# Second mixture of a fused attention and mixture kernel: the sixteen tiles of the seven-product form, in groups of four, four and eight in place of eight and eight

## The chip, the core and the metric

One core of one Trainium2 chip runs the whole program in one launch. The metric is the device time in microseconds (us) of that launch, from the first instruction to the last. TensorE is written PE (its weight loads PEld), VectorE DVE, ScalarE ACT, GpSimd POOL, and the queue of the sync engine SP.

## What is computed

Three stages follow each other: an attention with a feature map, a mixture in which each token goes to one of eight experts, and a second mixture in which every token goes through all four experts. The change touches the last one, which is this:

```python
def _moe2_ref(x, domain_probs, w1, w2) -> np.ndarray:
    N, D = x.shape                       # 2304, 512
    E = w1.shape[0]                      # 4; w1 is (4, 512, 1024), w2 is (4, 1024, 512)
    p = domain_probs / (domain_probs.sum(-1, keepdims=True) + 1e-09)
    out = np.zeros((N, D), dtype=np.float32)
    for e in range(E):
        h = np.maximum(x @ w1[e], 0.0)
        out += p[:, e:e + 1] * (h @ w2[e])
    return out.astype(np.float32)
```

## The kernel before

Tokens stand in 18 tiles of 128 rows. Every float32 operand is split into two float16 parts, hi and lo, and a product of two operands is three matmuls (hi·hi, hi·lo, lo·hi). The first layer of an expert can be done in two forms. Tiles 0 and 1 ("few") take the plain form, `few_l1` (matmuls at L1578, 256 columns). The other sixteen take a form with seven products of half-sized blocks in place of eight: tiles are paired, one from the first half of a group and one from the second, and from each pair seven block operands are made (`x2_two`), split in hi and lo, and turned by DMA transposes into `xq` (L1527). A group is a list of first tiles and a list of second tiles; before, there are two groups, tiles 2 to 9 and tiles 10 to 17, four tile pairs each (`GT = 4`), so a matmul of the form (L1595) has 512 columns.

An expert e runs as a list of units: the few unit, then one unit per group (`run_few`, `run_pair`). In a group's unit four steps j = 0 to 3 each issue the seven products of `pair_l1` (seven times six matmuls), and behind step j stands the second layer of step j - 1 for the group's first tiles (`l2_a`, L1638 with `ha`); the second tiles follow at the end (`l2_all`, L1638 with `hb`, 24 matmuls a tile), and each finished tile goes through `out_tile` (L1628 for expert 0, L1630 after). ACT copies the first product out of PSUM (L1601); DVE adds the others (L1603 to L1620); the hidden layer is rectified on ACT (L1567) and its low part made on DVE (L1568). Products rotate through four PSUM buffers (`psf`), so PE can stand four products ahead of the engines that empty them.

The order of the instructions on each engine is that of the code, and every engine takes its own in that order. Three things are interleaved with the units by counting: `x2.step(n)` advances the making of the next group's operands by n steps, `conv2.step(n)` advances the splitting of the expert's weights, and `x2.drain()` at the start of a unit puts all steps that are left there at once. Steps of `x2_pair` are taken in the few unit by the list `pace`, and in the first group's unit of expert 0 at each yield of `l2_a` (one or two steps in turn, one yield a tile and step j) and of `l2_all` (two steps, one yield a tile, behind the tile's `out_tile`). One tile pair takes six steps: norms on ACT (L160), scale factors on DVE (L166 to L170), scaling and the first split (L153, L1540 on ACT; L156, L1543, L1545, L1546 on DVE; a transpose of the operands A), the sums (L1549, L1550), and the second split (L1548, L1552 on ACT; L1553, L1555 on DVE; a transpose of the operands S). The first two tile pairs of the first group have norms and scales done earlier (`x2_norms`, `EARLY = 2`). The products of a step take operands in the order A11, A12, S2, S1, S3, S4, A22. A tile pair's operands need two `raw` buffers of six; weights wait in the same buffers.

## Time and profile before

| | us |
|---|---|
| median of three runs | 1328.69 (1323.92 to 1330.13) |
| the profiled execution | 1319.39 |
| its span, first to last instruction | 1317.6 |
| second mixture, from the few unit of expert 0 (592.7) to the last matmul (1311.1) | 718.4 |
| PE busy over the span | 1201.5 (91%) |
| DVE, ACT, POOL busy | 850.6, 566.9, 228.2 |
| mean granted clock of PE | 0.971 of full speed |

A matmul's row has its start, its length and, for an idle engine, how long PE sat before it and what ended that. [...]

### The profile page before, as it was taken

The page shows a single profiled execution, that of the slowest core. Times are in us where ns is not written, and L with a number is a line of the kernel's source. Part 1 is how long each engine was busy: PE and PEld are TensorE (multiplying, and loading weights), DVE is VectorE, ACT ScalarE, POOL GpSimd, SP SyncE. Part 2 cuts the span into 40 slices and gives each one's busy share as a digit, 9 for nine tenths or more (in the row PEclk, how much of TensorE's full clock was granted, in tenths as well). Part 3 has the DMA queues.
Part 4 walks back from the last instruction along what each step waited for, and adds up shares of the span by engine and source line. Part 5 has one row for each costly group of instructions (what it writes and reads, how often), then busy time and mean ns, then how long its engine had stood idle before and what let it go on. Part 6 is the DMA issues. An engine that isn't in the chain of part 4 may idle for free.

```text
span 1317.6 us, 19104 instructions
## 1 busy us (share of the span) xinstructions
PE 1201.5 (91%) x6889; PEld 672.4 (51%) x6889; DVE 850.6 (65%) x1817; ACT 566.9 (43%) x989; POOL 228.2 (17%) x298
## 2 busy tenths in 40 slices
PE   4899999646899999877999999999999999999998
PEld 2566667435375756534444454444454444544443
DVE  7979888764667777676785575437545368354451
ACT  5677857645465656554442442203323034221120
POOL 2534435132024432041000000000000000001102
PEclk9989989769899999999999999999999999999999
DMA  8788755289777676998044021000110001000001
GB/s 203 161 213 197 151 132 110 97 180 251 164 174 167 170 175 160 211 310 176 19 75 121 0 87 42 0 0 3 63 64 1 1 0 33 1 16 32 33 0 64
DMA packets 245450, 133.68 MB, mean 101 GB/s; under 512 B 196720, under 2 KB 225008, under 8 KB 245360
## 3 DMA queue, kind: packets, MB, share of 16 engines
q1 hardware_dynamic: 234784, 99.89, 33.8%
q0 software_dynamic: 9504, 31.01, 7.5%
q10 hardware_dynamic: 1072, 1.57, 0.4%
q8 instruction: 57, 0.93, 0.3%
q14 instruction: 33, 0.27, 0.1%
HBM read 69.45 MB, written 22.62 MB: 70 GB/s over the span
## 4 chain that ended last, share of the span: by engine, by line
issue 56%; PE 16%; DVE 12%; POOL 7%; DMA 5%; ACT 3%; SPq 1%; POOLq 0%; DVEq 0%; ACTq 0%
PE hp L1595 4%; PE num L743 3%; PE yp L1638 3%; PE kvb L668 3%; POOL wnr L150 2%; POOL raw L193 2%; POOL rec_scratch L1254 1%; POOL out_dram L1254 1%; DVE wr L156 1%; DVE x L156 1%; DMA qkT<-hv 1%; DMA xq<-raw 1%; PE pq L617 1%; PE kvb L669 1%; PE pk L621 1%
## 5 line engine op out<-in xcount | busy, mean ns | idle before, releaser
L1595 PE MATMUL hp<-xq,wr 128*128 128x512 f16 x1344 | 296.1, 380 | 7.2 <-DMA xq<-raw 4.9
L1595 PEld LDWEIGHTS <-wr 128*128 128x128 f16 x1344 | 131.7, 98 | 167.9 <-issue 5.6
L1638 PE MATMUL yp<-w2t,hb 128*128 128x512 f16 x960 | 209.9, 379 | 1.8 <-ACT hb L1567 1.7
L1376 PE MATMUL l1p<-wr,xsT 128*128 x1200 | 137.6, 276 | 45.9 <-DMA xsT<-xs_scratch 36.7
L1638 PE MATMUL yp<-w2t,ha 128*128 128x512 f16 x768 | 169.7, 379 | 0.0
L153 ACT ACTIVATE wr<-raw,n2s 128x1024 f16<-128x1024 f32 (+1 forms) x101 | 108.1, 1078 | 108.3 <-DVE n2s L169 58.5
L1638 PEld LDWEIGHTS <-hb 128*128 128x128 f16 x960 | 93.8, 98 | 115.1 <-ACT hb L1567 2.7
L1376 PEld LDWEIGHTS <-xsT 128*128 128x128 f16 x1200 | 118.8, 99 | 64.8 <-DMA xsT<-xs_scratch 36.9
L1402 PE MATMUL l2p<-wr,h 128*128 x600 | 137.1, 388 | 12.3 <-DVE y L1408 7.3
L1630 DVE SCALAR_TENSOR_TENSOR y<-yp,ce,y 128x512 f32<-128x512 f32 x54 | 40.5, 750 | 149.9 <-PE yp L1638 149.9
L156 DVE SCALAR_TENSOR_TENSOR wr<-raw,n2s,wr 128x1024 f16<-128x1024 f32 (+1 forms) x101 | 119.8, 1195 | 24.3 <-ACT wr L153 24.2
L1638 PEld LDWEIGHTS <-ha 128*128 128x128 f16 x768 | 75.1, 98 | 90.6
L1402 PEld LDWEIGHTS <-h 128*128 128x128 f16 x600 | 59.5, 99 | 88.5 <-issue 22.7
L1601 ACT ACTIVATE y<-hp 128x512 f32<-128x512 f32 x32 | 19.0, 594 | 186.8 <-PE hp L1595 186.8
L150 POOL PARTITION_ALL_REDUCE enr<-en x8 | 3.4, 426 | 535.0 <-ACT y L160 517.7
L1567 ACT ACTIVATE hb<-y 128x512 f16<-128x512 f32 x64 | 40.3, 630 | 120.3 <-DVE y L1612 99.8
L631 POOL PARTITION_ALL_REDUCE qp<-qp x36 | 73.0, 2030 | 103.1 <-ACT qp L626 103.1
L160 ACT ACTIVATE junk<-raw 128x1024 f32<-128x1024 f32 (+1 forms) x69 | 70.3, 1019 | 28.9 <-DMA raw<-in_moe_w_dram 25.8
L1603 DVE TENSOR_TENSOR y<-hp,y 128x512 f32<-128x512 f32 x32 | 22.1, 691 | 82.1 <-PE hp L1595 76.4
L150 POOL PARTITION_ALL_REDUCE wnr<-wn x61 | 33.4, 548 | 211.5 <-ACT junk L160 211.5
L743 PE MATMUL num<-kv,qp 128*128 128x65 f32 (+1 forms) x512 | 66.9, 286 | 3.0 <-DVE kv L727 3.0
L668 PE MATMUL kvb<-kp,vm 128*65 128x256 f32 x256 | 67.0, 408 | 2.6 <-DMA vm<-in_v_dram 2.4
(280 smaller groups left out, 1609.7 us busy)
## 6 DMA issues: line engine op xcount, KB each, us to landing
raw<-in_moe_w_dram SPq DMA_DIRECT2D x58, 512.0 KB, 3.7
raw<-in_moe_w_dram POOLq DMA_DIRECT2D x32, 512.0 KB, 5.1
xs_scratch<-junk SPq DMA_DIRECT2D x25, 256.0 KB, 3.4
y_scratch<-y SPq DMA_DIRECT2D x24, 256.0 KB, 3.3
rqk<-in_q_dram SPq DMA_DIRECT2D x16, 256.0 KB, 3.0
rqk<-in_k_dram SPq DMA_DIRECT2D x16, 256.0 KB, 3.4
vm<-in_v_dram SPq DMA_DIRECT2D x32, 128.0 KB, 3.2
rqk<-in_moe_w_dram SPq DMA_DIRECT2D x3, 512.0 KB, 8.0
```

Source lines behind the costliest of these rows:

```text
L150: nc.gpsimd.partition_all_reduce(o, i, P, bass_isa.ReduceOp.add)
L153: ACT(out=o, in_=i, func=AF.Copy, scale=sc)
L156: STT(out=o, in0=i, scalar=sc, in1=hi, op0=MUL, op1=SUB)
L160: ACT(out=junk, in_=i, func=AF.Square, accum_out=o)
L631: nc.gpsimd.partition_all_reduce(qt[:, 1, :], qt[:, 0, :], P, bass_isa.ReduceOp.absmax)
L668: nc.tensor.matmul(ps[0:D + 1], lhsT=vt[:, h % 4, t, :], rhs=kt[:, :, t, :], start=(t == 0), stop=False)
L743: nc.tensor.matmul(ps[:, t, :], lhsT=qt[:, f, t * P:(t + 1) * P], rhs=kvs[b][:, h, f, 0:w], start=(f == 0), stop=(f == 1))
L1376: nc.tensor.matmul(ps[:, s_, :], lhsT=xsT[j][:, xa_ * KD + c, :], rhs=win[c * 2 + wa], start=(m == 0), stop=(m == 3 * KD - 1))
L1402: nc.tensor.matmul(ps, lhsT=h[:, j % 2, ha, f, :], rhs=window(wt, off[j] + 2 * (f * 2 + wa) * DM, DM), start=(m == 0), stop=(m == 3 * FC - 1))
L1595: nc.tensor.matmul(ps, lhsT=wh[:, wi + c, wa, cols], rhs=xq[g][:, xi, xa_, c, :], start=(m == 0), stop=(m == 5))
L1630: STT(out=acc[T], in0=ps, scalar=ce_t[e][:, T:T + 1], in1=acc[T], op0=MUL, op1=ADD)
L1638: nc.tensor.matmul(ps, lhsT=h[:, ha, i * P:(i + 1) * P], rhs=w2t[:, f, wa, :], start=(first and m == 0), stop=(last_ and m == 2))
```

## The change

The list of groups is written out with 2, 2 and 4 tile pairs: tiles 2 to 5, 6 to 9 and 10 to 17. In the first two groups every matmul of the seven products has 256 columns in place of 512, and each of the additions, rectifications and copies behind it has 256 elements; there are twice as many. The second layer is the same 24 matmuls of 512 columns per tile. The gathers of tiles are the same ones at the same places (`NG2` stands for the 10 that was there), and the next expert's loads are freed at the same place, before the group of tiles 10 to 17. Steps of `x2` are now also taken in the second group's unit of expert 0.

```diff
-    halves2 = [(list(range(i, i + GT)), list(range(i + GT, i + 2 * GT))) for i in range(2, NTILE, 2 * GT)]
+    halves2 = []
+    for n_ in (GT // 2, GT // 2, GT):
+        i_ = len(few) + 2 * sum(len(h[0]) for h in halves2)
+        halves2.append((list(range(i_, i_ + n_)), list(range(i_ + n_, i_ + 2 * n_))))
...
-        xq = [f1.tile([P, 7, 2, 2, GT * P], F16, name=f"xq{i}") for i in range(len(halves2))]
+        xq = [f1.tile([P, 7, 2, 2, len(h[0]) * P], F16, name=f"xq{i}") for i, h in enumerate(halves2)]
...
-            yield from rounds((x2_two(g, i, inv) for i in range(GT)), True)
+            yield from rounds((x2_two(g, i, inv) for i in range(n)), True)
...
-                ps = psf.tile([P, GT * P], F32, name="hp", tag="hp")
+                ps = psf.tile([P, GT * P], F32, name="hp", tag="hp")[:, 0:N]
...
-                for i in range(GT):
+                for i in range(n):
                     for k in range(2):
                         l2_mm(yp[i], has[j][:, k], j + k * NQ, i, j + k == 0, j == NQ - 1 and k == 1)
...
-                if e == 0 and ui == 1:
+                if e == 0 and ui:
                     x2.drain()
-                    x2.add(x2pairs[1])
-                if e == 0 and ui == 2:
-                    x2.drain()
-                    conv2.free.add(("load", 1))
+                    if ui < len(x2pairs):
+                        x2.add(x2pairs[ui])
+                    else:
+                        conv2.free.add(("load", 1))
...
-                        if e == 0 and ui == 1 and ("w1", 0, 1) in conv2.ready:
+                        if e == 0 and ("w1", 0, 1) in conv2.ready:
                             x2.step(2 if kind > 1 else 1 + nstep % 2)
```

The order of the two programs shows what this moves at two places. In the rows the tile's own number stands in its name (y9 is tile 9, y17 tile 17), `yp` is the PSUM of the second layer, `hp` that of a product, and the lines of the changed kernel are four to six higher.

DVE in expert 0, around the last tile (tile 9) ahead of the unit of tiles 10 to 17, before:

```order
L1290 TENSOR_TENSOR coef_8062<-rec2_8059,yi1_8862 128x16
L1628 TENSOR_SCALAR y7_3354<-yp_9213,ce0_8426 128x512
L1628 TENSOR_SCALAR y8_3355<-yp_9239,ce0_8426 128x512
L1628 TENSOR_SCALAR y9_3356<-yp_9265,ce0_8426 128x512
L1603 TENSOR_TENSOR y22_3369<-hp_9300,y21_3368 128x512
```

The same place now:

```order
L1634 TENSOR_SCALAR y9_3356<-yp_9509,ce0_8422 128x512
L1559 TENSOR_TENSOR raw_9233<-y10_3357,raw_9233 128x2x256
L1557 TENSOR_TENSOR raw_9252<-y15_3362,raw_9252 128x2x256
L1553 SCALAR_TENSOR_TENSOR y12_3359<-y12_3359,n2s_9440,y16_3363 128x256
L1554 SCALAR_TENSOR_TENSOR y12_3359<-y12_3359,n2s_9440 128x256
L156 SCALAR_TENSOR_TENSOR raw_9453<-y13_3360,n2s_9503,raw_9453 128x2x256
L1547 TENSOR_TENSOR raw_9453<-y17_3364,raw_9453 128x256
L1549 TENSOR_TENSOR y17_3364<-y17_3364 128x256
L1550 SCALAR_TENSOR_TENSOR y17_3364<-y13_3360,n2s_9503,y17_3364 128x256
L1559 TENSOR_TENSOR raw_9252<-y11_3358,raw_9252 128x2x256
L1557 TENSOR_TENSOR raw_9348<-y16_3363,raw_9348 128x2x256
L1553 SCALAR_TENSOR_TENSOR y13_3360<-y13_3360,n2s_9503,y17_3364 128x256
```

Before, the operands of tiles 10 to 17 are complete ahead of tile 7's evacuation, and the next unit's additions follow tile 9's at once; now fifteen instructions that make operands of tiles 10 to 17 stand behind tile 9's evacuation (the last four of them, L1554, L1559, L1557 and L1559, are not shown), and the next unit's additions behind those.

ACT in expert 0, from the last rectification of step j = 1 to the copy of the first product of step j = 2, in the unit in which the operands of tiles 10 to 17 are begun; before (the first group):

```order
L1567 ACTIVATE hb_8423<-y20_3367 128x512
L160 ACTIVATE raw_8863,yn_8865<-y10_3357 128x2x256
L160 ACTIVATE raw_8863,yn_8865<-y14_3361 128x2x256
L153 ACTIVATE y14_3361<-y14_3361,n2s_8870 128x512
L153 ACTIVATE raw_8863<-y10_3357,n2s_8870 128x2x256
L1540 ACTIVATE raw_8863<-y14_3361 128x256
L160 ACTIVATE raw_8882,yn_8884<-y11_3358 128x2x256
L160 ACTIVATE raw_8882,yn_8884<-y15_3362 128x2x256
L153 ACTIVATE y15_3362<-y15_3362,n2s_8900 128x512
L153 ACTIVATE raw_8882<-y11_3358,n2s_8900 128x2x256
L1540 ACTIVATE raw_8882<-y15_3362 128x256
```

Now (the second group):

```order
L1572 ACTIVATE hb_8418<-y22_3369 128x256
L160 ACTIVATE raw_9232,yn_9234<-y10_3357 128x2x256
L160 ACTIVATE raw_9232,yn_9234<-y14_3361 128x2x256
L153 ACTIVATE y14_3361<-y14_3361,n2s_9245 128x512
L153 ACTIVATE raw_9232<-y10_3357,n2s_9245 128x2x256
L1544 ACTIVATE raw_9232<-y14_3361 128x256
L160 ACTIVATE raw_9251,yn_9253<-y11_3358 128x2x256
L160 ACTIVATE raw_9251,yn_9253<-y15_3362 128x2x256
L1607 ACTIVATE y19_3366<-hp_9257 128x256
```

Seven instructions stand there in place of ten, behind a step whose products are half as long; the first group's unit now has five at this place, for its own next group.

## Rows read from the trace of the kernel before

**Rows 1.** PE by time: start, us, instruction, count, idle before and what ended it.

```profile
598.29 2.78 PE L1578 MATMUL hp<-x2T,wr 128*128 128x256 f16 x24 [1.51 <-DVE hb L1568]
...
609.95 7.54 PE L1638 MATMUL yp<-w2t,hb 128*128 128x512 f16 x33 [1.45 <-ACT hb L1567]
622.35 4.42 PE L1595 MATMUL hp<-xq,wr 128*128 128x512 f16 x12 [4.86 <-DMA xq<-raw]
627.39 15.70 PE L1595 MATMUL hp<-xq,wr 128*128 128x512 f16 x72 [0.63 <-issue]
642.93 5.34 PE L1638 MATMUL yp<-w2t,ha 128*128 128x512 f16 x24
648.11 5.34 PE L1595 MATMUL hp<-xq,wr 128*128 128x512 f16 x24
654.97 4.04 PE L1595 MATMUL hp<-xq,wr 128*128 128x512 f16 x18 [1.52 <-ACT y L1601]
```

**Rows 2.** The same view later, where PE has no gap.

```profile
704.49 18.29 PE L1595 MATMUL hp<-xq,wr 128*128 128x512 f16 x84
722.62 5.34 PE L1638 MATMUL yp<-w2t,ha 128*128 128x512 f16 x24
...
782.19 10.64 PE L1578 MATMUL hp<-x2T,wr 128*128 128x256 f16 x96
792.67 10.52 PE L1638 MATMUL yp<-w2t,hb 128*128 128x512 f16 x48
```

**Rows 3.** By stretch: busy us and count of PE, PEld, DVE, ACT, POOL; granted clock; DMA.

```profile
622.00:627.00 5.00, 4.42 (x12) 1.46 (x12) 2.08 (x8) 0.60 (x1) 0.00 (x0) 0.66 1.08 201
627.00:643.00 16.00, 15.61 (x73) 7.15 (x74) 13.74 (x22) 5.60 (x9) 0.00 (x0) 1.00 0.00 1
...
704.00:782.00 78.00, 78.00 (x364) 35.35 (x362) 50.84 (x76) 30.17 (x46) 0.86 (x2) 1.00 0.10 32
...
803.00:880.00 77.00, 77.00 (x358) 34.94 (x357) 35.74 (x58) 16.56 (x28) 0.43 (x1) 1.00 0.00 1
```

**Rows 4.** Transposes to xq: SP's issue times, and landing (first all sixteen, then the two issued around 622).

```profile
L1527 SPq DMA_TRANSPOSE xq<-raw x16: 1420/1772/2987, 597.3 to 691.3; - x16
...
DMA to landing us min/median/max: 3.7/4.4/7.0
...
L1527 SPq DMA_TRANSPOSE xq<-raw x2: 1773/2168/2564, 620.5 to 622.4; - x2
...
DMA to landing us min/median/max: 4.5/4.7/4.9
```

**Rows 5.** ACT by time: a wait for a transpose in the few unit; then around 646 to 655.

```profile
605.84 0.63 ACT L1548 ACTIVATE raw<-y 128x512 f16<-128x512 f32 x1 [4.57 <-DMA xq<-raw]
...
646.27 0.61 ACT L160 ACTIVATE raw<-y 128x512 f16<-128x512 f32 x1
...
650.54 0.61 ACT L160 ACTIVATE raw<-y 128x512 f16<-128x512 f32 x1
...
654.35 0.57 ACT L1601 ACTIVATE y<-hp 128x512 f32<-128x512 f32 x1
```

**Rows 6.** DVE groups by form, 590 us to the end: count, busy us, mean ns of one.

```profile
L1568 DVE SCALAR_TENSOR_TENSOR hb<-y,hb 128x512 f16<-128x512 f32 x64 | 43.9, 687 | 3.1
...
L1568 DVE SCALAR_TENSOR_TENSOR hb<-hp,hb 128x256 f16<-128x256 f32 x32 | 13.1, 418 | 11.1 <-ACT hb L1567 11.1
```

**Rows 7.** DVE by time, the end of the first group's operands (thirteen instructions, four shown).

```profile
614.12 0.68 DVE L1555 TENSOR_TENSOR raw<-y,raw 128x512 f16<-128x512 f32 x1
...
618.31 0.69 DVE L1553 TENSOR_TENSOR raw<-y,raw 128x512 f16<-128x512 f32 x1 [0.61 <-ACT raw L1548]
...
620.43 0.68 DVE L1553 TENSOR_TENSOR raw<-y,raw 128x512 f16<-128x512 f32 x1
621.04 0.68 DVE L1555 TENSOR_TENSOR raw<-y,raw 128x512 f16<-128x512 f32 x1
```

More of the change, by code (lines that the diff above doesn't have):

```diff
@@ L282, in tile_linear_attention_moe_moe2 @@
     HD = DM // 2
+    NG2 = 10
     few = list(range(2))
-    halves2 = [(list(range(i, i + GT)), list(range(i + GT, i + 2 * GT))) for i in range(2, NTILE, 2 * GT)]
+    halves2 = []
+    for n_ in (GT // 2, GT // 2, GT):
+        i_ = len(few) + 2 * sum(len(h[0]) for h in halves2)
+        halves2.append((list(range(i_, i_ + n_)), list(range(i_ + n_, i_ + 2 * n_))))
     B11, B12, T1, T3, T2, T4 = 0, 4, 8, 10, 12, 14
@@ L1479, in tile_linear_attention_moe_moe2 @@
             C2 = {0: 0, 1: 1, 2: 1, 3: 1}
-            GA = {j: [j - 9] for j in range(9, 19)}
-            X2 = {12: 1, 13: 1, 15: 1, 16: 1, 18: 1, 19: 1, 20: 1, 22: 1, 24: 1}
+            GA = {j: [j - 9] for j in range(9, 9 + NG2)}
+            X2 = {12: 1, 13: 1, 15: 1, 16: 1, 18: 1, 19: 1, 20: 1, 22: 1}
             for j in range(NSLOT):
@@ L1559, in x2_pair @@
             inv = xinv if g == 0 else f1.tile([P, GT, 2], F32, name=f"yi{g}")
-            yield from rounds((x2_two(g, i, inv) for i in range(GT)), True)
+            n = len(halves2[g][0])
+            yield from rounds((x2_two(g, i, inv) for i in range(n)), True)
             for k in range(2):
-                coefs(halves2[g][k][0], inv[:, :, k], GT)
+                coefs(halves2[g][k][0], inv[:, 0:n, k], n)
             yield
@@ L1587, in pair_l1 @@
             wh = conv2.w1[j // 2]
+            N = len(halves2[g][0]) * P
             cols = slice(j % 2 * P, (j % 2 + 1) * P)
             def product(xi, wi):
-                ps = psf.tile([P, GT * P], F32, name="hp", tag="hp")
+                ps = psf.tile([P, GT * P], F32, name="hp", tag="hp")[:, 0:N]
                 m = 0
@@ L1598, in product @@
                 return ps
-            t, c, u, v, w = [fu() for _ in range(5)]
+            t, c, u, v, w = [fu()[:, 0:N] for _ in range(5)]
             ACT(out=t, in_=product(A11, B11), func=AF.Copy)
@@ L1603, in pair_l1 @@
             TT(out=c, in0=product(A12, B21), in1=t, op=ADD)
-            low = hidden(ha[0], c)
+            low = hidden(ha[0], c, N)
             yield
@@ L1612, in pair_l1 @@
             TT(out=w, in0=p7, in1=v, op=ADD)
-            low = hidden(hb_[1], w)
+            low = hidden(hb_[1], w, N)
             TT(out=u, in0=p7, in1=u, op=ADD)
@@ L1617, in pair_l1 @@
             low()
-            low = hidden(ha[1], v)
+            low = hidden(ha[1], v, N)
             yield
@@ L1621, in pair_l1 @@
             low()
-            low = hidden(hb_[0], u)
+            low = hidden(hb_[0], u, N)
             yield
@@ L1666, in run_pair @@
             ta_, tb_ = halves2[g]
+            n = len(ta_)
             yp = None
@@ L1687, in run_pair @@
                     conv2.need(("w2", e))
-                    coef_e(e, ta_[0], 2 * GT)
-                    yp = [psf.tile([P, DM], F32, name="yp", tag="yp") for _ in range(GT)]
+                    coef_e(e, ta_[0], 2 * n)
+                    yp = [psf.tile([P, DM], F32, name="yp", tag="yp") for _ in range(n)]
                 yield from l2_a(j - 1)
@@ L1694, in tile_linear_attention_moe_moe2 @@
         conv2.need(("norms", 1, 0))
-        for T in range(2 * GT + len(few), NTILE):
+        for T in range(NG2, NTILE):
             gather(T, acc)
@@ L1701, in tile_linear_attention_moe_moe2 @@
         x2.add(x2pairs[0])
-        pace = iter([2, 2, 1, 2, 1, 2, 0, 0, 99])
+        pace = iter([3, 2, 1, 2, 1, 2, 0, 0, 99])
         for e in range(E2):
```

## The prediction

> **What bounds the kernel now.** I read the busy time by stretch first, then PE by time, then what ended its gaps. From 704 us to the end of the second mixture PE has no gap at all: 78.00 us busy of 78.00 and 77.00 of 77.00 in the two stretches shown, at the full granted clock, with DVE at 50.84 and 35.74 [rows 3]. There only the number and length of matmuls counts. Before that, in expert 0, PE waits. Its time line shows where: in the few unit, where the gaps are ended by DVE and ACT; at 622.35, where it has sat 4.86 us until a transpose of the first group's operands landed; at 627.39, where its third product starts just after the last of those transposes landed (issued 622.37, 4.9 us to landing: 627.3); and at 654.97, where ACT's copy of a product came late [rows 1, 4]. What a smaller first group can remove is the wait at 622 to 627. What it adds must be looked for in the same 100 us, and in the length of the matmuls.
>
> **The matmuls.** A steady stream of 512 columns goes from 704.49 to 722.62 with 84 matmuls, 18.13/84 = 215.8 ns each; one of 256 columns, with the same 128x128 weights, from 782.19 to 792.67 with 96, 109.2 ns each [rows 2]. Per expert, 168 matmuls of 512 (36.25 us) become 336 of 256 (36.69 us): 0.44 us, times four experts **+1.8 us**. A unit of four tiles then takes 36.69/2 + 96 x 0.2158 = 39.1 us when nothing waits.
>
> **The start of the first group.** The few unit's last matmul ends at 617.49 (609.95 + 7.54) and the third product begins at 627.39; two products of six matmuls are 12 x 0.2158 = 2.6 us, so 7.3 us are lost there (the granted clock of 0.66 in that stretch costs nothing more, since the two products end before the last landing) [rows 1, 3]. Now four transposes are needed and not eight. The first two are issued as before, at 597.3 and shortly after 600. The last tile pair's second half still waits until the second of them has landed, as ACT did until 605.84 [rows 5], since its buffer is the same; add two ACT splits, two DVE splits and 4.4 to 4.9 us of landing [rows 4, 6]: about 612.5. The few unit cannot end by then: its last rectifications stand behind that same ACT instruction. I walk them through to 609.1 and its last matmul to 616.9, which is 0.6 us earlier than now. So the operands are there in time, and the term is -7.3 - 0.6 = **-7.9 us**. Its bounds: -6 if the few unit ends no earlier and a landing is 1.3 us late, -10.5 if the few unit loses none of the 3 us that its gaps show.
>
> **The steps behind the last tile of the second group.** This is the term that turns the sum. Tiles 10 to 17 are four tile pairs, so 4 x 6 + 1 = 25 steps. Before, a unit with four first tiles offered 16 yields of one or two steps and four of two, 24 + 8 = 32, and all were done ahead of tile 7. Now the unit in which they are made has two first tiles: 8 yields make 12 steps, and two make 4: 16. Nine steps are left to the drain, and two more belong to the last yield, behind tile 9. The order shows the result: fifteen DVE instructions behind tile 9's evacuation. DVE takes its instructions in turn, so none of them can start before PE has finished the group; call that moment T. Their price: the thirteen instructions from 614.12 to 621.72 are the same sequence less one L1553 and one L1555, with one bubble of 0.6 us [rows 7]: 7.6 - 0.6 + 2 x 0.6 = 8.2 us. Ahead stands the evacuation of tile 9, 0.7 us; so the last DVE split ends at T + 8.9. The last transpose follows the one before it, which holds SP for some 1.8 us, at about T + 9.5, and lands 4.9 us later [rows 4]: T + 14.4. PE may run its first two products when the operands A are in, but the third needs the last landing, as it did at 627.39. Without a wait it would start at T + 2.6. The term is **+11.8 us**. What could hide it is the unit's own work, and there is none: the next unit is the group itself. Bounds: 10 (no queueing, 3.7 us to landing) and 14.5 (7.0 us to landing).
>
> **Shorter cover for ACT and DVE in expert 0.** Between the last product of a step and the moment PE runs out of PSUM buffers stand the second layer of the step before (6 matmuls a first tile) and four products. Before that is 5.2 + 5.2 = 10.4 us; in a group of four tiles 2.6 + 2.6 = 5.2 us. What must fit is the work on ACT ahead of the copy L1601. Before, it did not quite fit: from PE's last product at 642.9 to the end of L1601 at 654.92 it is 12.0 us, and PE sat 1.52 us [rows 1, 5]. One tile pair's part is 650.54 - 646.27 = 4.3 us, norms alone some 1.6, and ACT began 3.2 us behind PE [rows 5]. In the first group's unit now: two additions and two splits of weights fall in each of the first two steps, beside 22 evacuations; at 0.38 us apiece (418 ns of which some 0.04 to 0.08 overlap [rows 6]) that is 8.4 + 4.0 us in a PE time of 9.2, and PE gets 1.8 us behind beyond what four buffers hold. Then one tile pair (4.3 us) behind a lag of some 4 us: 8.3 against 5.2, 3.1 us lost. At the next step 1.4. In the second group's unit there are no weights, the lag is about 1.3; a tile pair and one set of norms, with the copy 0.4: 7.0 to 8.5 against 5.2 to 7, 1.5 us, and at the next step 3.3, since DVE scales one pair before it gives ACT the factors of the next. Together 11.1, in place of the 2.0 lost before (steps from 648 to 673): **+9.2 us**. This is an estimate by hand from those rows, and the weakest of the terms: bounds -2 (nothing waits any more, and PE's stream before has only those 2.0 us to give) and +13.
>
> Experts 1 to 3 I put at nothing: in 803 to 880 DVE is busy 35.74 of 77 us [rows 3], and the weights' splitting falls on the last unit, whose shape is unchanged. POOL and its gathers keep their order, and SP has nothing but the sixteen transposes until the loads behind them. The tail behind the last group is unchanged.
>
> A row against this change: half the elements do not halve an evacuation. It is 687 ns at 128x512 and 418 at 128x256 [rows 6], so 176 evacuations of 512 (one group, 4 steps x 4 experts x 11) become 352 of 256, 352 x 0.418 - 176 x 0.687 = +26.2 us of DVE time. I count it as covered outside expert 0. [...]
>
> **The sum.** +1.8 - 7.9 + 11.8 + 9.2 = +14.9 us on a span of 1317.6: 1332.5; with the 1.8 us around the span the profiled execution would be 1334.3 in place of 1319.39. The three runs of before have a median 9.3 us above that execution; I add the difference to the median: 1328.7 + 14.9 = 1343.6, or **1343**.
>
> **The rivals.**
> 1. The cover suffices: ACT and DVE lose no more in expert 0 than before, the third term is 0. Then +5.7, 1334. For it: before, a batch of two tile pairs cost PE only 1.5 us. Against it: cover is halved and the batch is not.
> 2. The change does what it says, and the tail behind tile 9 is hidden: +1.8 - 7.9 = -6.1, 1323, not slower. It would need the eight transposes to land within 2.6 us of T, thus DVE to get to those fifteen instructions ahead of tile 9's evacuation. The order speaks against it; only if PE were so late in the second group that DVE and ACT had drained in the meantime would a part be saved, and the order forbids even that.
> 3. DVE becomes the bound of the 256-column steps in all experts: 11 x 418 ns = 4.6 us stands against 42 x 109.2 ns = 4.6 us of PE [rows 2, 6]. Where the second layer between the steps does not make it up, the added 26.2 us of DVE come out at PE: with the other terms less the third, +5.7 + 26 = +32, 1361. Against it: overlap between neighbours, and 2.6 us of second layer behind each step but the first.
>
> **How the numbers follow.** My forecast (all four terms) 0.62; the first rival 0.16; the second 0.08; the third 0.05; the rest, 0.09, is for a few unit or a clock that goes otherwise by some us. A difference of over 0.5%, 6.6 us, is about what a measurement of this kernel can tell from none. The forecast and the third rival are slower by more; so is a part of the first rival's spread and of the rest: 0.74. The first rival's centre (+5.7) and the second's (-6.1) lie within: 0.20. Faster by more takes the second rival with a few unit that loses nothing: 0.06. The terms' bounds give +1.8 - 10.5 + 10 - 2 = -0.7 to +1.8 - 6 + 14.5 + 13 = +23.3; they will not all lie at one end, and the median of a few runs moves by some 3 us. The range takes the first rival in and leaves out the second and third: 1331 to 1352.
>
> **What would show it.** In the trace of after: PE's first 256-column product within 0.3 us of the few unit's end near 617, with no gap ended by a transpose; a stream of 256 columns at 109 ns; the unit of tiles 2 to 5 ending near 662 and that of tiles 6 to 9 near 706; there a gap of 8 to 9 us ended by a transpose, a granted clock below full as at 622, and a second wait of which the end is the last landing, near 720; from there to the end PE without a gap in experts 1 to 3. I am wrong if that gap is short or missing, if PE's gaps in the first two units come to less than 4 us, or if units of four tiles take much over 39.1 us in experts 1 to 3.

## The result, and the profile after

The changed kernel takes 1339.45 us (median of 4 runs, 1335.15 to 1341.43). The kernel before took 1326.31 us beside it (4 runs, 1320.88 to 1330.13). The ratio is 1.0109, with a 95% interval of 1.0059 to 1.0158: it is slower by more than 0.5%. The prediction was 1343 us, 1331 to 1352. It stands on a median of 1328.69 for the kernel before, of three runs; with the fourth run the two medians differ by 13.1 us, where the forecast has 14.9. The profiled execution took 1335.15 us, its span is 1333.4 us, and the prediction's sum for these two was 1334.3 and 1332.5.

PE by time in expert 0, after (start, us, instruction, count; in brackets the idle time before and what ended it). The rows answer to [rows 1] and [rows 2].

```profile
604.56 10.52 PE L1644 MATMUL yp<-w2t,hb 128*128 128x512 f16 x48
614.92 8.15 PE L1601 MATMUL hp<-xq,wr 128*128 128x256 f16 x72
624.10 1.47 PE L1601 MATMUL hp<-xq,wr 128*128 128x256 f16 x12 [1.03 <-DVE y L1609]
...
631.33 1.26 PE L1601 MATMUL hp<-xq,wr 128*128 128x256 f16 x10 [1.64 <-DVE wr L156]
633.60 2.12 PE L1601 MATMUL hp<-xq,wr 128*128 128x256 f16 x18 [1.01 <-ACT y L1607]
...
642.33 2.12 PE L1601 MATMUL hp<-xq,wr 128*128 128x256 f16 x18 [1.39 <-ACT y L1607]
...
659.83 9.33 PE L1601 MATMUL hp<-xq,wr 128*128 128x256 f16 x84
...
675.50 2.12 PE L1601 MATMUL hp<-xq,wr 128*128 128x256 f16 x18 [1.13 <-ACT y L1607]
...
685.59 3.79 PE L1601 MATMUL hp<-xq,wr 128*128 128x256 f16 x18 [2.75 <-ACT y L1607]
...
694.40 10.52 PE L1644 MATMUL yp<-w2t,hb 128*128 128x512 f16 x48
712.75 4.56 PE L1601 MATMUL hp<-xq,wr 128*128 128x512 f16 x12 [7.82 <-DMA xq<-raw]
720.18 17.20 PE L1601 MATMUL hp<-xq,wr 128*128 128x512 f16 x72 [2.88 <-DMA xq<-raw]
...
807.28 10.52 PE L1644 MATMUL yp<-w2t,hb 128*128 128x512 f16 x48
```

The wait for transposes at the first group is gone: its first product starts where the few unit's last matmul ends. In its place stand three things: six short gaps in the two units of four tiles (four ended by ACT's copy of a product, two by DVE), a gap of 7.82 us ahead of the last group, and a second one of 2.88 us two products later. From 720.18 to the end PE does not wait again.

The same by stretch, as in [rows 3] (busy us and count of PE, PEld, DVE, ACT, POOL; granted clock; DMA share; GB/s):

```profile
705.00:712.00 7.00, 0.00 (x0) 0.10 (x1) 6.86 (x14) 1.86 (x5) 0.00 (x0) 0.83 0.71 129
...
725.00:797.00 72.00, 72.00 (x336) 32.67 (x335) 47.60 (x73) 28.94 (x44) 0.87 (x2) 1.00 0.14 49
818.00:895.00 77.00, 77.00 (x524) 51.07 (x522) 39.07 (x104) 20.33 (x48) 0.43 (x1) 1.00 0.01 1
```

From 705 to 712 DVE works through and PE does nothing: that is the tail. In expert 1's two units of four tiles (818 to 895) PE has no gap, although DVE is busy 39.07 us there, against 35.74 in [rows 3].

DVE by time around the end of the second group. The first row is tile 9's evacuation, the last one the fifteenth instruction behind it:

```profile
704.96 0.75 DVE L1634 TENSOR_SCALAR y<-yp,ce 128x512 f32<-128x512 f32 x1 [2.10 <-PE yp L1644]
705.63 0.68 DVE L1559 TENSOR_TENSOR raw<-y,raw 128x512 f16<-128x512 f32 x1
...
713.05 0.68 DVE L1559 TENSOR_TENSOR raw<-y,raw 128x512 f16<-128x512 f32 x1
```

**How the runs below are compared.** The stages ahead of the second mixture end some us earlier or later from run to run: the few unit's last matmul ends between 610 and 618 us in most profiles here, and at 622.9 and 624.5 in two. So I measure a stretch of PE's time: from the end of the few unit's last matmul in expert 0 to its end in expert 1. Before, it runs from 609.95 + 7.54 [rows 1] to 792.67 + 10.52 [rows 2]: 185.70 us. After, it runs from 604.56 + 10.52 to 807.28 + 10.52: 202.72 us, which is 17.0 more. Without a wait it would be 176.2 before (two units of 77.70, the few unit 20.84) and 176.7 after (two units of 39.06, one of 77.70, the few unit). So the waits in it, with what the clock costs behind them, come to 9.5 us before and 26.1 after. Each stretch is read from one profile; the two profiles of the kernel after differ by 1.9 us in it, so a difference of about 2 us between two kernels tells little by itself.

### The profile page after: what moved, and what is told of

It is laid out like the page before. It is cut to its first block, busy times and chain, and to the rows that moved or that the text cites. A ratio compares the mean times of both kernels' runs of the same rounds, so it can differ in the third digit from the quotient of the medians.

```text
span 1333.4 us, 20812 instructions
## 1 busy us (share of the span) xinstructions
PE 1207.3 (91%) x7561; PEld 742.0 (56%) x7561; DVE 862.9 (65%) x2005; ACT 581.2 (44%) x1069; POOL 232.0 (17%) x298
## 4 chain that ended last, share of the span: by engine, by line
issue 55%; PE 19%; DVE 9%; POOL 7%; DMA 5%; ACT 3%; SPq 1%; POOLq 0%; DVEq 0%; ACTq 0%
PE num L747 4%; PE yp L1644 3%; PE kvb L672 3%; PE hp L1601 3%; POOL wnr L150 2%; POOL raw L193 2%; DMA raw<-in_moe_w_dram 1%; DVE wr L156 1%; POOL out_dram L1258 1%; POOL rec_scratch L1258 1%; PE kvb L673 1%; PE pq L621 1%; PE pk L625 1%; DMA qkT<-hv 1%; DMA y_scratch<-y 1%
## 5 line engine op out<-in xcount | busy, mean ns | idle before, releaser
L1601 PE MATMUL hp<-xq,wr 128*128 128x256 f16 (+1 forms) x2016 | 303.9, 311 | 19.7 <-DMA xq<-raw 10.7
L1601 PEld LDWEIGHTS <-wr 128*128 128x128 f16 x2016 | 198.7, 99 | 124.2 <-issue 24.2
L1406 PE MATMUL l2p<-wr,h 128*128 x600 | 134.5, 382 | 14.8 <-DVE y L1412 11.6
L156 DVE SCALAR_TENSOR_TENSOR wr<-raw,n2s,wr 128x1024 f16<-128x1024 f32 (+1 forms) x101 | 119.8, 1195 | 24.6 <-ACT wr L153 24.4
L1607 ACT ACTIVATE y<-hp 128x256 f32<-128x256 f32 (+1 forms) x48 | 21.6, 450 | 183.5 <-PE hp L1601 183.5
L1572 ACT ACTIVATE hb<-y 128x256 f16<-128x256 f32 (+1 forms) x96 | 46.8, 487 | 121.5 <-DVE y L1618 102.8
L1609 DVE TENSOR_TENSOR y<-hp,y 128x256 f32<-128x256 f32 (+1 forms) x48 | 24.6, 513 | 81.6 <-PE hp L1601 70.8
L1572 ACT ACTIVATE ha<-y 128x256 f16<-128x256 f32 (+1 forms) x96 | 46.8, 487 | 64.6 <-DVE y L1609 46.4
L150 POOL PARTITION_ALL_REDUCE wnr<-wn x61 | 36.2, 593 | 206.2 <-ACT junk L160 206.2
```

The costliest lines, as they stand in the source:

```text
L150: nc.gpsimd.partition_all_reduce(o, i, P, bass_isa.ReduceOp.add)
L156: STT(out=o, in0=i, scalar=sc, in1=hi, op0=MUL, op1=SUB)
L1406: nc.tensor.matmul(ps, lhsT=h[:, j % 2, ha, f, :], rhs=window(wt, off[j] + 2 * (f * 2 + wa) * DM, DM), start=(m == 0), stop=(m == 3 * FC - 1))
L1572: ACT(out=o[:, 0, 0:n], in_=ps, func=AF.Relu)
L1601: nc.tensor.matmul(ps, lhsT=wh[:, wi + c, wa, cols], rhs=xq[g][:, xi, xa_, c, :], start=(m == 0), stop=(m == 5))
```

## The experiments

All runs were timed beside the kernel before on the same chip. The table has the stretch from each profiled execution, what it has over the 185.70 us of before, and the measured ratio. From there to the last matmul, experts 1 to 3 add 1.3 us to every kernel with groups of four or six except the one with eight, four, four, where they add 9.2 because the later few units wait too.

| Kernel | Stretch, us | Over before | Median, us | Ratio and 95% interval |
|---|---|---|---|---|
| after | 202.72 | +17.0 | 1339.45 | 1.0109 [1.0059, 1.0158] |
| after, again | 200.84 | +15.1 | 1338.21 | 1.0125 [1.0081, 1.0168] |
| steps only in the second layer | 198.65 | +13.0 | 1329.42 | 1.0103 [1.0066, 1.0141] |
| last steps ahead of the evacuations | 197.34 | +11.6 | 1326.60 | 1.0054 [1.0019, 1.0088] |
| groups of eight, four, four | 201.34 | +15.6 | 1344.24 | 1.0173 [1.0101, 1.0245] |
| one step a yield | 200.51 | +14.8 | 1335.45 | 1.0119 [1.0020, 1.0218] |
| steps moved; four, four, eight | 191.32 | +5.6 | 1326.21 | 1.0041 [1.0014, 1.0068] |
| steps moved; four, six, six | 187.86 | +2.2 | 1322.39 | 1.0011 [0.9986, 1.0036] |
| the same, loads held back | 185.02 | -0.7 | 1318.61 | 1.0008 [0.9988, 1.0029] |
| the same, input steps later | 187.25 | +1.5 | 1320.53 | 1.0026 [1.0001, 1.0051] |
| four, six, six, loads held, more conversion | 183.48 | -2.2 | 1315.24 | 0.9991 [0.9966, 1.0016] |
| four, four, eight, loads held back | 184.07 | -1.6 | 1313.56 | 0.9990 [0.9956, 1.0023] |

**Are the six gaps a matter of where the input steps stand?** The forecast put them down to two things: the splitting of weights in the first unit, and batches of one tile pair's input work, queued on ACT ahead of the copy of the next step's first product, with half the former cover. ACT by time ahead of the gaps at 675.50 and 685.59, after:

```profile
670.22 0.61 ACT L160 ACTIVATE raw<-y 128x512 f16<-128x512 f32 x1
...
672.17 0.72 ACT L153 ACTIVATE y<-y,n2s 128x512 f32<-128x512 f32 x1 [0.50 <-DVE yi L170]
...
674.46 0.63 ACT L160 ACTIVATE raw<-y 128x512 f16<-128x512 f32 x1
...
675.09 0.37 ACT L1607 ACTIVATE y<-hp 128x256 f32<-128x256 f32 x1
...
682.27 0.72 ACT L153 ACTIVATE y<-y,n2s 128x512 f32<-128x512 f32 x1 [2.81 <-DVE yi L170]
...
685.18 0.36 ACT L1607 ACTIVATE y<-hp 128x256 f32<-128x256 f32 x1
```

Ahead of the longer gap ACT first waits 2.81 us for scale factors that DVE makes behind another pair's work, which the forecast named as its reason.

The first experiment gives the input steps to the yields of the units' second layer alone:

```diff
-                            x2.step(2 if kind > 1 else 1 + nstep % 2)
+                            x2.step({32: 4, 33: 4, 34: 4, 35: 4, 36: 9}.get(nstep, 0))
```

> The changed kernel, but in the two units of four tiles of expert 0 no step of the next operands is taken between the four steps j; they are all taken behind step j = 3, four at each yield of the second layer there and nine behind the third tile. Work and matmuls are the same. Theory (the batches on ACT and DVE do not fit under the halved cover of 5.2 us): the gaps ended by ACT's copy of a product, 6.3 us in four places in the changed kernel, and the half clock behind the longest of them go; the two gaps of the first unit that the splitting of weights causes (1.0 and 1.6) stay; the tail behind tile 9 gets some 2 us shorter, as one step set less stands behind it. Span 1333.4 - 8 - 2 = 1323 to 1326. Rival (256-column products are simply too quick for ACT and DVE, whatever else they do): the gaps inside the units stay within 2 us of their sum, span 1330 to 1333.

PE by time in that kernel, first and second group and the start of the third:

```profile
621.39 1.47 PE L1601 MATMUL hp<-xq,wr 128*128 128x256 f16 x12 [1.03 <-DVE y L1609]
...
634.28 4.75 PE L1601 MATMUL hp<-xq,wr 128*128 128x256 f16 x42
...
658.72 9.61 PE L1601 MATMUL hp<-xq,wr 128*128 128x256 f16 x72 [2.84 <-DMA xq<-raw]
...
670.75 4.75 PE L1601 MATMUL hp<-xq,wr 128*128 128x256 f16 x42
...
687.69 10.52 PE L1644 MATMUL yp<-w2t,hb 128*128 128x512 f16 x48
705.88 4.65 PE L1601 MATMUL hp<-xq,wr 128*128 128x512 f16 x12 [7.67 <-DMA xq<-raw]
713.33 17.29 PE L1601 MATMUL hp<-xq,wr 128*128 128x512 f16 x72 [2.80 <-DMA xq<-raw]
```

All four gaps that the copy L1607 ended are gone. Those at 621.39 and one of 1.65 us stay; they go only in kernels below that move steps of the weights' conversion. But the steps now end later, and the second group waits 2.84 us for a transpose of its own. The tail is as long as in the kernel after: the third product starts 15.1 us after the second group's last matmul (687.69 + 10.52). I had expected 2 us less there, and that was a miss. Moving the steps bought 4.1 us of the stretch (2.2 against the second profile of the kernel after), where I had forecast some 10, and the ratios, 1.0103 beside 1.0109 and 1.0125, do not tell the two kernels apart. So this run shows what made the gaps of the copy, but no gain in time that the ratios could tell.

A second kernel gives one step to each yield of the second group's unit, in place of one or two:

```diff
-                            x2.step(2 if kind > 1 else 1 + nstep % 2)
+                            x2.step(2 if kind > 1 else 1 + (nstep % 2 if ui == 1 else 0))
```

> The changed kernel, but in the second group's unit one step at each yield of the second layer in place of one and two in turn: 8 + 4 = 12 steps of 25 there, thirteen left over in place of nine. Theory: both terms trade against each other. The gaps inside the unit (1.1 and 2.8 us, and the half clock behind) shrink to about 1 to 2 us, and the tail grows by four steps of 0.7 to 2 us on DVE: the last landing at T + 18 to T + 20 in place of T + 15.3. Span within 3 us of the changed kernel's 1333.4. Rival (the tail is set by the transposes alone): the tail stays at T + 15.3 and the span falls by 3 to 4 us.

PE by time, the second unit's j = 2 and 3 and the third group's start:

```profile
679.41 4.75 PE L1601 MATMUL hp<-xq,wr 128*128 128x256 f16 x42
...
686.59 4.75 PE L1601 MATMUL hp<-xq,wr 128*128 128x256 f16 x42
...
718.53 4.39 PE L1601 MATMUL hp<-xq,wr 128*128 128x512 f16 x12 [11.66 <-DMA xq<-raw]
```

The second unit runs dense and the tail grows: the first of its gaps is 11.66 us in place of 7.82, and the third product starts 19.1 us behind the second group. So the size of the batch makes the gaps of that unit, and the steps left over make the tail. One is traded for the other: the stretch and the ratio are those of the kernel after within the scatter.

**Is the tail DVE's order?** Here the leftover steps are issued ahead of the evacuations of tiles 8 and 9 (`out_tile`), and nothing else changes:

```diff
+                if ahead:
+                    x2.step(ahead[i])
                 out_tile(e, T, ps)
...
-            yield from l2_all(e, tb_, hb)
+            yield from l2_all(e, tb_, hb, (7, 99) if e == 0 and g == 1 else None)
```

> The changed kernel, but in the second group's unit of expert 0 the steps that are left stand ahead of the evacuations of tiles 8 and 9 on DVE (seven and the rest), not behind. Theory (the fifteen instructions are late because they stand behind an evacuation that waits for PE): DVE works through the second layer of tiles 8 and 9, and the last transpose lands at about T + 10 in place of T + 15.3, T being PE's last matmul of the group; the second half-clock stretch behind it goes. Span 1333.4 - 5 - 1.5, 1326 to 1329; more is not had, since DVE has some 18 us of such work from the end of step j = 3 on against 15.6 us of PE. Rival (landing of the transposes, not DVE's order, sets the wait): the wait stays within 1 us, span 1332 to 1335.

PE by time:

```profile
702.92 2.75 PE L1601 MATMUL hp<-xq,wr 128*128 128x512 f16 x12 [1.30 <-DMA xq<-raw]
710.29 18.62 PE L1601 MATMUL hp<-xq,wr 128*128 128x512 f16 x72 [4.62 <-DMA xq<-raw]
```

The two gaps of 7.82 and 2.88 become 1.30 and 4.62. The third product starts 8.7 us after the second group's last matmul, in place of 15.3, and the gaps inside the units are unchanged. I had also expected the slow stretch behind it to go (a granted clock of 0.50 from 720 to 723 in the kernel after), and that was a miss: the 72 matmuls there take 18.62 us, against 17.20 in the kernel after and 15.70 in the kernel before, at a granted clock of 1.00 [rows 1, 3]. So the place of the steps behind an evacuation that waits for PE made the larger part of the tail, 6.6 of 12.7 us beyond the two products. What is left is work and transposes for eight tiles that come after the cover is used up.

**Is the first group's wait a matter of its size?** Groups of eight, four and four:

```diff
-    for n_ in (GT // 2, GT // 2, GT):
+    for n_ in (GT, GT // 2, GT // 2):
```

> The groups in the order eight, four, four tiles (2 to 9, 10 to 13, 14 to 17), all else as in the changed kernel: the same 256-column matmuls and evacuations in every expert, but the first group is as large as in the kernel before, and the 13 steps for each next group fit their unit (32 and 16). Theory: the start of the first group costs what it did before (PE waits 4.9 us and then some 2.4 for transposes), no tail stands behind any group, the eight-tile unit loses less than the 2.0 us of before, the first unit of four some 2 to 5 us, and the matmuls 1.8. Span 1317.6 + 1.8 + 1 to 4: 1320 to 1324, ratio to the kernel before 1.002 to 1.005. Rival (groups of four cost in every expert): 1330 or more.

PE by time at the first group, and at expert 1's few unit:

```profile
627.73 4.18 PE L1601 MATMUL hp<-xq,wr 128*128 128x512 f16 x12 [3.20 <-DMA xq<-raw]
...
797.05 0.39 PE L1583 MATMUL hp<-x2T,wr 128*128 128x256 f16 x2 [3.10 <-ACT wr L153]
...
806.93 7.64 PE L1583 MATMUL hp<-x2T,wr 128*128 128x256 f16 x48 [4.48 <-DVE hb L1573]
```

The wait is back with eight tiles in front (3.20 us ahead of the first product, 1.18 more ahead of the third), and there is no tail; both were expected. The time was not: I had forecast 1320 to 1324 us, a gain over the changed kernel, and this has the highest ratio of all, though its interval overlaps that of the kernel after. The next expert's weights are converted under the last unit, and a last unit of four tiles has half the time and half the yields for that. Expert 1's few unit takes 34.5 us instead of 20.8. I had looked at the inputs alone and not at what else the last unit hides.

**Can the split be made to pay?** The next kernels take the waits away one after the other. First the steps are moved: five of the second group's steps and four of the conversion's (in place of three between the first group's products) go ahead of the few unit's second layer, the others to the second layer behind j = 3 of the unit before, and expert 1's loads are freed as soon as the last input is prepared. One kernel has the change's groups, one has groups of four, six and six (`(2, 3, 3)`); in the first of them the steps are:

```diff
+        takes = {0: {0: 3, 1: 2, 2: 1, 3: 2, 4: 1, 5: 2, 8: 5}, 1: {32: 4, 33: 4, 34: 4, 35: 4}, 2: {32: 5, 33: 4, 34: 4, 35: 4, 36: 4}}
...
+                        if ui == 0 and nstep == 8:
+                            conv2.step(4)
+                        x2.step(takes.get(ui, {}).get(nstep, 0))
+                        if ui == 2 and not x2.todo:
+                            conv2.free.add(("load", 1))
```

The kernel after ran once more beside them.

> The changed kernel itself once more, beside the next two and the same runs of the kernel before. Every theory: ratio to the kernel before 1.008 to 1.014; in its profile the same gaps as in the first one (third product of tiles 10 to 17 at T + 15.3, T being PE's last matmul of tiles 6 to 9; gaps ended by ACT of 6.3 us in all), whatever the stages ahead of the second mixture do.

> The changed groups (four, four, eight tiles), with the steps where neither PE nor a full PSUM waits for them: the weights' second half and five steps under the few unit's second layer, all other steps behind j = 3 of the two units of four tiles, those for tiles 10 to 17 begun one unit earlier (16 + 21 steps, 25 of them theirs, none left over); the next expert's loads are freed when they are done. Same matmuls, evacuations and transposes. Theory (the whole loss of the changed kernel is where the steps stand, and only 1.8 us is in the smaller products): from the few unit's last matmul to expert 1's first one 156 to 159 us, where the kernel before has 164.9 and the changed one 181.9; no gap at tiles 10 to 17; ratio to the kernel before 0.992 to 0.998. Rival (DVE has too much to do in the first 80 us, wherever it stands): gaps come back elsewhere, and these two units take 85 us or more in place of 78.1; 165 us or more, ratio 1.00 or above.

> Groups of four, six and six tiles, products of 256, 384 and 384 columns, with the steps placed as in e6: 19 for the second group (five under the few unit's second layer, fourteen in the first unit), 19 for the third, all in the units' ends. Theory: same first group, so the same start; matmuls cost the same 0.44 us an expert; DVE has more room; 156 to 158 us from the few unit's last matmul to expert 1's first. In experts 1 to 3 the last unit has six tiles, so fewer steps for the next expert's weights, which cost in e3 where it had four: 0 to 3 us a boundary. Ratio to the kernel before 0.992 to 1.000. Rival (weights become late as in e3): gaps at the few units of experts 1 to 3 of over 3 us each, ratio above 1.00.

The repeat gave what it gave before. The two others took away most of the loss, but neither was faster than before, and both missed their forecast (0.992 to 0.998 and 0.992 to 1.000): the first is measurably slower at 1.0041, the second the same at 1.0011. PE by time in the one with four, four and eight, and then ACT by time there:

```profile
700.43 4.43 PE L1601 MATMUL hp<-xq,wr 128*128 128x512 f16 x12 [2.57 <-DMA xq<-raw]
709.73 15.26 PE L1601 MATMUL hp<-xq,wr 128*128 128x512 f16 x60 [4.86 <-ACT y L1607]
```

```profile
702.35 1.06 ACT L160 ACTIVATE y<-raw 128x1024 f16<-128x1024 f32 x1 [9.49 <-DMA raw<-in_moe_w_dram]
...
708.04 1.06 ACT L160 ACTIVATE y<-raw 128x1024 f16<-128x1024 f32 x1 [1.45 <-DMA raw<-in_moe_w_dram]
...
709.10 0.58 ACT L1607 ACTIVATE y<-hp 128x512 f32<-128x512 f32 x1
```

The new gap is of my own making. The loads were freed earlier, and four norms of expert 1's weights came to stand on ACT ahead of the third group's first copy. ACT sat 9.49 us in front of the first of them, whose load had not landed, and PE stopped for 4.86 us after 24 matmuls, four products, which fill the four PSUM buffers. With six and six tiles it is the same, with 9.60 us on ACT and a gap of 2.72 us on PE. The next kernels leave out the early freeing, alone and with the five input steps moved into the first group's unit:

```diff
-                        if ui == 2 and not x2.todo:
-                            conv2.free.add(("load", 1))
```

> Groups of four, six and six tiles with the moved steps (the kernel of the run before), and one thing taken back: the loads for expert 1's weights are asked for again only at the start of the third unit, not as soon as the last input is prepared. In the run before, ScalarE stood 9.60 us in front of a norm of expert 1's weights whose load had not landed, and the copy of the third group's first product (L1607), queued behind four such norms, came at 721.67, which left TensorE a gap of 2.72 us, one of 0.84 us and a clock at half for 6.8 us. Theory (the copy is late only because the norms stand ahead of it on ScalarE): both gaps and the half clock go, some 7 us, so the stretch from the few unit's end to expert 1's first product falls from 167.0 to about 160 us, and the ratio from 1.001 to 0.994 to 0.998. Rival (ScalarE and VectorE are late there for the inputs themselves): a gap of 2 us or more stays at the third group's start and the ratio stays within 0.001 of 1.001.

> As the kernel before in this job, and besides, the five input steps of the second group that stood ahead of the few unit's second layer go into the second layer of the first four-tile unit (two behind j = 1, three behind j = 2). They stood on ScalarE and VectorE ahead of the first group's first copy (L1607 at 618.57, where its product had ended near 616.2), ahead of a gap of 2.63 us. Theory (the first copy waits behind those steps): the gap of 2.6 us falls under 1 us, the later steps find cover in 512-column matmuls, and the wait for the second group's transposes grows from 0.96 to under 2 us: 1 to 2 us less than the kernel before. Rival (the gap is set by the norms of the second weights, which stand there too): the gap stays over 1.5 us, and the time is the same or 1 to 2 us longer by the later transposes.

Without the early freeing, both gaps at the third group are gone and the part of the stretch up to expert 1's first product falls from 167.0 to 160.2 us, as the theory had it. The whole stretch falls by less, 2.8 us, since the conversion now comes late and expert 1's few unit takes 24.8 us, and the ratio of 1.0008 (forecast 0.994 to 0.998) can't be told from the 1.0011 of the run before. PE by time in expert 1's few unit:

```profile
776.71 5.40 PE L1583 MATMUL hp<-x2T,wr 128*128 128x256 f16 x48 [1.26 <-DVE hb L1573]
782.59 0.59 PE L1644 MATMUL yp<-w2t,hb 128*128 128x512 f16 x2 [0.48 <-ACT w2t L153]
783.91 0.81 PE L1644 MATMUL yp<-w2t,hb 128*128 128x512 f16 x3 [0.73 <-DVE w2t L156]
```

With the input steps later, the first group's gap of 2.61 us went, as expected, and one of 2.76 us came four products into j = 3; the second group's wait grew from 0.98 to 1.85 us. The stretch was worse by 2.2 us, where I had forecast a gain of 1 to 2: the copy's wait moved to another place and did not go. Last, the six-and-six kernel gets seven further conversion steps under its last unit, and the early freeing goes from the kernel with the change's own groups:

```diff
+                    if e == 0 and ui == 3 and nstep in (6, 15, 16, 25, 26, 35, 36):
+                        conv2.step()
```

> As the kernel that asks for expert 1's loads at the start of the third unit (groups of four, six and six), with seven further steps of expert 1's conversion in that unit (one after the third unit's first seven products, the others two at a time in the second layer of j = 1 to 3), so that by expert 1's few unit as many are done as with a last group of eight. In that kernel the stretch from the few unit's end to expert 1's first product was 160.2 us, but expert 1's few unit took 24.8 us in place of the 20.8 us of the kernel before: its second weights were converted inside it (waits of 1.26, 0.48, 0.73 and 0.72 us). Theory (all that is short there is conversion done by that point): the few unit comes down to 20.8 to 21.5 us and the stretch stays within 1 us of 160.2, so the two together are 181 to 182 us against 185.7 us of the kernel before, and the ratio is 0.996 to 0.999. Rival (the steps are work that ScalarE and VectorE have no room for under the last group either): new gaps of 2 us or more inside the third unit, and a ratio over 1.000.

> The change's own groups (four, four and eight) with the moved steps as in the earlier run of them, and expert 1's loads asked for only at the start of the third unit. In that earlier run ScalarE stood 9.49 us in front of a norm of expert 1's weights, the copy of the third group's first product came at 709.10, and TensorE had a gap of 4.86 us and its clock at half for 6.8 us behind it. Theory (head of line on ScalarE): that gap and that half clock go, the stretch from the few unit's end to expert 1's first product falls from 170.5 to 162 to 164 us, and since a last group of eight leaves four second-layer steps a turn instead of three, expert 1's few unit stays dense at 20.8 us: 183 to 185 us together against 185.7 us of the kernel before, a ratio of 0.998 to 1.001. Rival (eight tiles' worth of inputs are late in any case): the gap of 4.9 us is ended by a transpose instead, and the ratio stays at 1.003 to 1.005.

The first group of the kernel with more conversion:

```profile
622.76 8.38 PE L1601 MATMUL hp<-xq,wr 128*128 128x256 f16 x60 [2.62 <-ACT y L1607]
```

What PE still waits for between 600 and 820 us in the last of these (us in total, times, longest):

```profile
PE hp L1601 <- ACT y L1607: 2.6, 1, 2.6
PE hp L1601 <- DMA xq<-raw: 2.6, 1, 2.6
```

Expert 1's few unit is back at 20.8 us in both. The stretch of the last one, 184.07 us, is within its forecast; that of the other, 183.48, is 1.5 us over its 181 to 182. There the granted clock was 0.53 from 623 to 626.6, behind the copy's wait of 2.62 us, and 60 matmuls took 8.38 us; behind the same wait of 2.62 us in the last one they take 6.71, at a granted clock of 1.00 (616 to 620). Both stretches are some 2 us less than before, of which experts 1 to 3 take 1.3 back, and two profiles of one kernel differ by as much; the ratios of 0.9991 and 0.9990 can't be told from 1. A version that is measurably faster than the kernel before was not found. What the split brought is small: against 176.7 us without a wait, the two best orders still lose 6.8 and 7.4 us, where the kernel before loses 9.5.

## Why the prediction was right

Each term of the sum, against the two profiled executions. T is the end of the second group's last matmul, 704.92.

| Term | Predicted, us | Bounds | Measured |
|---|---|---|---|
| Stages ahead, to the few unit's start | 0 | | -0.7 |
| Start of the first group | -7.9 | -10.5 to -6 | -9.2 |
| Cover for ACT and DVE, with these units' matmuls (0.4) | +9.6 | -1.6 to +13.4 | +10.3 |
| Tail behind tile 9 | +11.8 | 10 to 14.5 | +14.2 |
| Matmuls of experts 1 to 3 | +1.4 | | +1.3 |
| Sum | +14.9 | | +15.9 |

The span grew by 15.8 us. The signs and the order of the terms are as forecast; that the sum came within 1 us is in part luck, since the errors of the terms cancel (start -1.3, tail +2.4), and the second profile of the same kernel has +8.7 for the cover and +14.0 for the tail, with a span of 1331.4 in place of 1333.4. The terms behind it:

- **Start.** The operands were there in time and the 7.5 us between the few unit and the first group are gone. The few unit itself, counted from its first matmul (588.18 before, not the 592.7 of the table in front), took 27.4 us in place of 29.2, which is 1.7 less where I had 0.6. That part is not shown to come from the change: in four more profiles of kernels with the same few unit it took between 27.4 and 30.7 us. Two small parts of the change act near there that its description in front leaves out: the last input step of the stage ahead (`X2`, entry 24) is gone from its place, and the few unit's list `pace` begins with three steps in place of two. No run tests them alone. That the wait belongs to the first group's eight tiles was shown by the kernel that puts eight in front.
- **Cover.** The two units of four tiles end at 659.83 and 704.92, near 662 and 706 as forecast, and take 90.0 us; before, the unit of eight took 82.1, less 2.45 for its wait, 79.7. Its mechanism was right: the kernel with the steps in the second layer took all four gaps of the copy away, the one with one step a yield those of the unit that it changed. Its size is in part luck. The losses of the hand count add up to 11.1 us (less 2.0 that is 9.1; the prediction has 9.2), while the six gaps measure 8.95: the first batch of the first unit cost 1.01 us where I had 3.1, and PE's 1.64 us ahead of 631.33 were a wait for the weights themselves (L156), not for a full PSUM. What made up for it is mainly the clock, which the forecast did not have there: the 18 matmuls behind 685.59 took 3.79 us, at a granted clock of 0.59 from 685 to 689, in place of 2.12.
- **Tail.** The last DVE split ended at 713.73, T + 8.8 (forecast T + 8.9). The last transpose was issued at 715.45, T + 10.5, one us later than I had it, since the transpose ahead, issued at 713.1, held SP for 2.2 us. The third product began at T + 15.3, not T + 14.4. The remaining 1.5 us are the clock: I had a granted clock below full during the two products of the gap (0.56 from 712 to 717), which costs nothing, since they end 2.88 us before the third can start, but not a second stretch below full behind the second wait (0.50 from 720 to 723): 72 matmuls in 17.20 us, where they take 15.70 at a granted clock of 1.00 [rows 1, 3]. The mis-sized step is this term, at 14.2 for 11.8, inside its bounds.
- **Matmuls.** In experts 1 to 3 the 256-column stream runs at 109.2 ns a matmul, from start to start, and a unit of four tiles takes 39.06 us, without gaps. The third rival (DVE as the bound there) is refuted by the row of 818 to 895 above.

The first rival, that the cover suffices, fails on the gaps in both units. The second, that the tail is hidden, fails on the 7.82 us (its sum of -6.1 also leaves out the cover term, which its condition does not touch); its condition (DVE comes to those instructions ahead of tile 9's evacuation) was tried on its own, and even then 1.30 and 4.62 us are left.

The clock, by stretch, behind the two waits (columns as above):

```profile
712.00:717.00 5.00, 4.25 (x12) 1.48 (x11) 2.23 (x7) 1.19 (x2) 0.00 (x0) 0.56 1.15 215
717.00:720.00 3.00, 0.30 (x2) 0.00 (x0) 0.69 (x1) 0.63 (x1) 0.00 (x0) 0.98 1.04 193
720.00:723.00 3.00, 2.81 (x7) 1.02 (x8) 0.06 (x1) 0.00 (x0) 0.00 (x0) 0.50 1.03 345
```

Over the 5 us with the two products between the waits the granted clock was 0.56 of full speed; it was 0.98 while PE waited again, and 0.50 in the 3 us in which the third product began.

## What to carry to other kernels

A smaller first group starts sooner (here by 9.2 us), but every piece of work that used to fall under the larger one (here input steps, weight conversion, loads) has to find a new place, and each must be counted with its own yields before the gain is. Where an engine takes its instructions in the order of the code, as DVE does here behind tile 9's evacuation (704.96 to 713.73) and ACT ahead of the third group's copy (9.49 us), look at the last evacuation of a stage and at what is queued behind it, and at the first copy of the next stage and what is queued ahead: together these cost PE more here (a tail of 14.2 us and four gaps of 6.3 in all) than the wait that was removed (7.5). Here five placements ended within 2.2 us of the old stretch: most of the waits had been exchanged for others.

## What the runs showed of the hardware

**Behind the same wait the granted clock was 0.59 in one run and 1.00 in another.** In the kernel after, PE waited 2.75 us ahead of 685.59, and the granted clock from 685 to 689 was 0.59; in its second profiled run the same wait took 2.8 us, and the clock there was 1.00. The stretch 685 to 689 in the first and in the second run:

```profile
685.00:689.00 4.00, 3.41 (x17) 2.47 (x17) 3.01 (x8) 1.66 (x6) 0.00 (x0) 0.59 0.00 0
```

```profile
685.00:689.00 4.00, 3.58 (x26) 2.53 (x26) 3.35 (x10) 1.66 (x7) 0.00 (x0) 1.00 0.00 0
```

In the same 4 us the one ran 17 matmuls and the other 26. The stretch of the table differs by 1.9 us between these two runs of one kernel, and this is the larger part of it. So what came behind a wait near 2.8 us cost nothing more or, by the 18 matmuls of the first run, 1.7 us more (3.79 less 2.12) in one and the same kernel, and a single profile does not fix it.

**Evacuations at a third size.** DVE by form in the kernel after, and then in the kernel with groups of six tiles:

```profile
L1573 DVE SCALAR_TENSOR_TENSOR hb<-y,hb 128x256 f16<-128x256 f32 x64 | 26.9, 420 | 4.5 <-ACT hb L1572 2.6
```

```profile
L1573 DVE SCALAR_TENSOR_TENSOR hb<-y,hb 128x384 f16<-128x384 f32 x64 | 35.4, 554 | 4.0
```

554 ns at 384 elements lies halfway between 420 at 256 and the 687 at 512 of [rows 6]: the three lie on a straight line. Carried on to no elements, the line leaves some 150 ns an instruction (420 less 267), an estimate from these three means; what that part is made of no run here shows.
